# The conditional block moved ahead of the last slot's scalings and scatters, and that slot's rows transposed by TensorE

## The chip, the cores and the metric

The kernel runs on one core of a Trainium2 chip. The metric is the device time of one execution in microseconds; of several executions the median is taken. A profiled execution also gives a span, from the first to the last instruction of the core, and a trace of that execution.

## What is computed

Attention with a causal mask and a decay bias runs over 8 batches of 8 heads (576 positions of 64 values). Its output, 4608 rows of 512 values, goes through a mixture of 16 experts (4 groups of 4), each of which has a hidden layer of 1024. A row goes to one expert, chosen by two argmax steps:

```python
x = attn_out.transpose(0, 2, 1, 3).reshape(B * S, H * D)      # 4608 x 512
g_idx = argmax(x @ w_group)                                   # group of a row, with softmax weight g_w
e_idx = argmax(x @ w_expert[g_idx])                           # expert in the group, with weight e_w
h = maximum(x_row @ w1[g, e], 0.0)                            # 512 -> 1024
out[row] = (g_w * e_w) * (h @ w2[g, e])                       # 1024 -> 512
```

## The kernel before

The first half of the execution is attention and routing; the change does not touch it. In the second half (`moe`) the 16 experts, sorted by how many rows they have, are handled in 16 slots, 0 to 15. A slot has a fixed capacity (`CAPS`): slot 13 has 264 rows, slots 14 and 15 have 256, so two tiles of 128 rows. Rows beyond a capacity go to the conditional block at the end, which is entered when the count `nov` is above zero. With these inputs it is not entered: no instruction of its body stands in the trace.

Each float32 matrix is split into a rounded high part and the low rest (`wh`, `wl`; `xh`, `xl`; `hh`, `hl`), and a product is three matmuls. A slot has these steps:

- `gather`: GpSimd fetches the slot's rows from DRAM into `xg` by an indirect DMA, long ahead.
- `x_items`: the rows are transposed and split into `xh` and `xl`. Slots 0 and 1 do it on TensorE, into PSUM (lines 1040 to 1045). All later slots do it on VectorE: 16 transposes of 32-row blocks into `xt` (line 1059), then a cast on ScalarE (`xh`, line 1063) and a subtraction on VectorE (`xl`, line 1064) for each half.
- `h_items`: 8 pieces of 12 matmuls (line 1092), each followed by `hh` on ScalarE (line 1087) and `hl` on VectorE (line 1088).
- `y_items`: where the capacity is a multiple of 128, `y_rows` (lines 1105 to 1124): 4 pieces of 12 matmuls of 512 columns (line 1114), two pieces to a tile of 128 rows. Behind the second piece of a tile VectorE scales the tile by the row's weight (line 1121), and GpSimd scatters it into the output (line 943).
- `z_items`: for other capacities, 16 transposes on VectorE (line 1200), three scalings on ScalarE (line 1203) and three scatters. They run during the next slot's `h_items`, and the scalings stand behind all 16 transposes.
- `load`: 16 pieces for the next slot's weights, with casts on ScalarE (lines 982 and 990) and subtractions on GpSimd (985) and VectorE (992).

Each engine runs its instructions in the order in which they stand. In the loop over the slots (lines 1433 to 1447) the order on TensorE, VectorE and ScalarE is the order of the code: pieces of the next slot's `x_items` and `load` stand between the pieces of this slot. GpSimd's and the DMA queues' order is the scheduler's. PSUM tiles come from two pools, `acc` for products and `turn_in` for transposes and casts; `turn_in` has four buffers, used in turn.

Behind the loop stands the block: every engine loads `nov` into a register (line 1449), compares and branches (line 1450). On the path around the body each engine raises its own semaphores by what the body would have raised them; GpSimd does this also for the eight semaphores of its DMA queue (`INC_SWDGE_SEM`). Behind it comes the end of the program: the Sync engine waits for all DMAs, and all five engines meet in a barrier, for which GpSimd first runs a `DRAIN`.

Of the kernel before, what the change touches and what calls it, by code (L numbers as in the profile page):

```python
# [13 lines left out]
ALU = mybir.AluOpType  # L14
# [8 lines left out]
DM = 512  # L23
FF = 1024
E = 16
# [883 lines left out]
def moe(tc, w1, w2, xs, st, out):  # L909
# [3 lines left out]
    with ExitStack() as ctx:  # L913
# [27 lines left out]
        def scatter(y, ids, free=False):  # L941

            i = nc.gpsimd.indirect_dma_start(out=out, in_=y, in_offset=None, bounds_check=NTOK - 1, oob_is_err=False,  # L943
                                             out_offset=bass.IndirectOffsetOnAxis(ap=ids, axis=0))
            if free:
                tc.declare_no_dep(i.ins, group="rows", reason="distinct rows")
                tc.add_to_no_dep_group("rows", i.ins)
# [52 lines left out]
        def turn_in(name, dt=F32):  # L1000

            n = turned_in[0] = turned_in[0] + 1
            return pt[n > 6 and n % 4 == 3].tile([P, 512], dt, name=name, tag="pt")
# [18 lines left out]
        class Slot:  # L1022
# [12 lines left out]
            def x_items(self):  # L1035
                u, cap = self.u, self.cap
                self.xh, self.xl = xhl(u, 0 if u == 0 else u + 1)

                def item(c):
                    ps = acc(f"px{u}_{c}") if u == 0 else turn_in(f"px{u}_{c}")  # L1040
                    for t, r in enumerate(self.rows):
                        nc.tensor.transpose(ps[:, t * P:t * P + r], self.xg[:r, t, c * P:(c + 1) * P], ident[:r, :r])
                    self.split = (nc.scalar.copy(self.xh[:, c, :cap], ps[:, :cap]),
                                  V.tensor_tensor(out=self.xl[:, c, :cap], in0=ps[:, :cap],
                                                  in1=self.xh[:, c, :cap].bitcast(F32), op=ALU.subtract))

                if u < 2:
                    return [lambda c=c: item(c) for c in range(4)]

                xt = turned(u)  # L1050
                nb = -(-cap // 32)

                def turn(j, i0):

                    n = len(range(j, nb, 4))
                    for i in (i0, i0 + 1):
                        src = self.xg[32 * j:32 * j + 32].rearrange("p t (c i n) -> p t c i n", c=4, n=32)
                        dst = xt[32 * i:32 * i + 32].rearrange("p c (t j n) -> p t c j n", j=4, n=32)
                        V.transpose(dst[:, 0:n, :, j], src[:, 0:n, :, i])  # L1059

                def split(a):
                    xh, xl, x = (t[:, a:a + 2, :cap] for t in (self.xh, self.xl, xt))
                    nc.scalar.copy(xh, x)  # L1063
                    V.tensor_tensor(out=xl, in0=x, in1=xh.bitcast(F32), op=ALU.subtract)  # L1064

                return ([lambda j=j, i=i: turn(j, i) for j in range(4) for i in (0, 2)] +
                        [lambda a=a: split(a) for a in (0, 2)])
# [37 lines left out]
            def y_rows(self):  # L1105

                pss, yr = {}, {}

                def item(t, f0):
                    if f0 == 0:  # L1110
                        pss[t] = acc(f"py{self.u}_{t}")
                    for f in range(f0, f0 + 4):
                        for n, (x, w) in enumerate(((self.hh, self.w.h), (self.hh, self.w.l), (self.hl, self.w.h))):
                            nc.tensor.matmul(pss[t], x[:, f, t * P:(t + 1) * P], w[2 + f // 4][:, f % 4],
                                             start=(f == 0 and n == 0), stop=(f == 7 and n == 2))
                    if f0 == 4:
                        if t == 0:
                            yr[0] = rows(self.u) if self.u % 2 else yT.rearrange("p c t -> p (c t)").rearrange(
                                "p (t d) -> p t d", d=DM)
                        yo = yr[0][:, t]  # L1120
                        V.tensor_scalar(out=yo, in0=pss[t], scalar1=self.cw[:, t:t + 1], scalar2=None, op0=ALU.mult)
                        scatter(yo, self.ids[:, t:t + 1], True)

                return [lambda t=t, f=f: item(t, f) for t in range(len(self.rows)) for f in (0, 4)]

# [83 lines left out]
        class Tile:  # L1209
# [8 lines left out]
            def items(self):  # L1218
# [17 lines left out]
                def hidden(i, c0):  # L1236
                    if c0 == 0:

                        pss[i] = turn_in(f"pu{u}_{i}") if u == "r" else acc(f"pu{u}_{i}")
                    for c in range(c0, c0 + 2):  # L1240
                        for n, (a, b) in enumerate(((th, w.h), (tl, w.h), (th, w.l))):
                            nc.tensor.matmul(pss[i], a[:, c, 0:P], b[i][:, c], start=(c == 0 and n == 0),
                                             stop=(c == 3 and n == 2))
                    if c0 == 2:
                        nc.scalar.activation(h[:, i * 512:(i + 1) * 512], pss[i], AF.Relu)
# [4 lines left out]

                def y(f0):
                    if f0 == 0:
                        pss["y"] = acc(f"pv{u}")
                    for f in range(f0, f0 + 2):
                        fs = slice(P + P * (f % 2), 2 * P + P * (f % 2))
                        for n, (a, b) in enumerate(((th, w.h), (tl, w.h), (th, w.l))):
                            nc.tensor.matmul(pss["y"], a[:, f // 2, fs], b[2 + f // 4][:, f % 4],
                                             start=(f == 0 and n == 0), stop=(f == 7 and n == 2))
                    if f0 == 6:
                        yo = rows(u)[:, 0]  # L1260
                        V.tensor_scalar(out=yo, in0=pss["y"], scalar1=self.cw, scalar2=None, op0=ALU.mult)
                        scatter(yo, self.ids)
# [171 lines left out]
        with tc.manual_schedule(engines={ENG.PE, ENG.DVE, ENG.Activation}):  # L1434
            for k in range(1, E):
                W = wts[k + 1].load() if k + 1 < E else []
                for i, f in enumerate(slots[k].h_items()):
                    f()
                    run(Z[i:i + 1] + W[i:i + 1])
                    if i == 4 and k + 2 < E:  # L1440
                        slots[k + 2].gather()
                X = slots[k + 1].x_items() if k + 1 < E else []
                for i, f in enumerate(slots[k].y_items()):
                    run((Z[8:] if i == 0 else []) + X[4 * i:4 * i + 4] + W[8 + 2 * i:10 + 2 * i])
                    f()
                Z = slots[k].z_items()
            run(Z)

        nov = nc.values_load(spilli[0:1, 3:4], min_val=0, max_val=2 * E)  # L1449
        with tc.If(nov > 0):  # L1450
# [54 lines left out]
            with tc.If(nge > 0):  # L1505
# [50 lines left out]
                with tc.For_i(0, nge, 1) as i:  # L1556
# [8 lines left out]
                    run(w.load())  # L1565
                    run(o.items())


def _layout(inputs):
    import numpy as np  # L1570
# [41 lines left out]
```

## Time and profile before

| | us |
|---|---|
| median of 3 runs (lowest, highest) | 950.84 (948.24, 955.85) |
| the profiled execution | 953.42 |
| its span | 951.7 |
| TensorE busy | 869.3 (91% of the span) |
| VectorE busy | 747.3 (79%) |
| ScalarE busy | 609.0 (64%) |
| GpSimd busy | 606.6 (64%) |

The mean granted TensorE clock is 0.963 of full speed. Busy times are summed over the whole span; the change concerns its last 55 us. Times in rows are microseconds from the start of the span. A number in square brackets at the end of a row is the idle time of that engine just ahead of the instruction, with what ended it. Rows whose engine name ends in "q" are instructions that an engine's queue handles itself (branches, register loads, semaphores, drains); they do not count as busy.

### The profile page before, as it was taken

How to read it: one execution, taken by the hardware profiler on the slowest of the kernel's cores; microseconds unless marked ns; L12 is line 12 of the kernel's file. 1: busy time of each engine (PE TensorE's matmuls, PEld its weight loads, DVE VectorE, ACT ScalarE, POOL GpSimd, SP SyncE). 2: the span in 40 equal slices, each digit the busy share in tenths (PEclk: the TensorE clock that was granted, in tenths of full speed). 3: DMA queues.
4: the chain of work that ended last, by engine and by line, in shares of the span. 5: the costliest groups of instructions: out<-in, count | busy, mean ns of one | idle time of the engine just before them, and what ended most of it. 6: DMA issues, size and time to landing. Idle time of an engine off the chain costs nothing. (4 is left out here: it accounts for less than half of the span.)

```text
span 951.7 us, 17736 instructions
## 1 busy us (share of the span) xinstructions
PE 869.3 (91%) x5576; PEld 792.1 (83%) x5576; DVE 747.3 (79%) x1996; ACT 609.0 (64%) x1383; POOL 606.6 (64%) x748
## 2 busy tenths in 40 slices
PE   4889899999899999999695999999999999999983
PEld 3678788888788888887584999999999999999972
DVE  7546688787988788775599678898888889888850
ACT  5458668677767767775634556767677666676640
POOL 9647567666666757546675557666676777676630
PEclk9979999999999999998797999999999999999997
DMA  7999989989999989712536345556555555565410
GB/s 189 229 196 225 221 213 227 221 200 200 212 210 213 216 213 226 175 57 103 196 125 212 137 160 190 186 167 223 185 200 188 205 190 176 212 223 208 145 43 23
DMA packets 82165, 174.65 MB, mean 184 GB/s; under 512 B 9708, under 2 KB 45164, under 8 KB 73872
## 3 DMA queue, kind: packets, MB, share of 16 engines
q1 hardware_dynamic: 71952, 153.52, 58.7%
q0 software_dynamic: 7488, 18.89, 5.6%
q10 hardware_dynamic: 2624, 1.03, 0.5%
q8 instruction: 46, 0.75, 0.4%
q14 instruction: 55, 0.45, 0.2%
HBM read 108.97 MB, written 19.69 MB: 135 GB/s over the span
## 5 line engine op out<-in xcount | busy, mean ns | idle before, releaser
L985 POOL TENSOR_TENSOR wl<-raw,wh 128x512 fp32r<-128x512 f32 x163 | 209.9, 1300 | 76.0 <-ACT wh L982 57.3
L221 DVE CUSTOM_DVE_ANT_0 mx<-pm,mask 128x192 bf16<-128x192 f32 (+4 forms) x320 | 127.5, 419 | 46.7 <-PE pm L213 44.1
L982 ACT CAST wh<-raw 128x512 fp32r<-128x512 f32 x256 | 155.2, 616 | 11.6 <-issue 11.6
L1092 PE MATMUL ph<-xl,wh 128*128 128x256 f32 (+13 forms) x512 | 146.7, 306 | 4.0 <-DVE xl L1064 4.0
L1092 PE MATMUL ph<-xh,wh 128*128 128x256 f32 (+13 forms) x512 | 145.8, 303 | 3.9 <-ACT xh L1063 3.8
L213 PE MATMUL pm<-WA 66*128 66x288 f32 (+4 forms) x384 | 127.8, 364 | 22.6 <-DVE mc L221 12.0
L269 PE MATMUL ps<-WA 68*128 68x320 f32 (+4 forms) x384 | 138.4, 364 | 3.0 <-ACT pu L279 1.9
L309 PE MATMUL po<-pt,VT 128*128 128x256 f32 (+3 forms) x512 | 123.8, 362 | 8.1 <-ACT sums L316 6.8
L1147 PE MATMUL py<-hl,wh 128*128 128x256 f32 (+13 forms) x448 | 113.7, 302 | 1.9 <-DVE hl L1088 1.9
L1147 PE MATMUL py<-hh,wh 128*128 128x256 f32 (+13 forms) x448 | 112.8, 301 | 0.0
L1059 DVE STREAM_TRANSPOSE xt<-xg 32x256 f32<-32x256 f32 (+1 forms) x224 | 109.4, 489 | 3.4
L271 PE MATMUL ps<-WB 128*128 128x320 f32 (+4 forms) x384 | 112.0, 305 | 0.0
L309 PE MATMUL po<-pu,VT 128*128 128x320 f32 (+1 forms) x384 | 109.7, 395 | 0.3 <-POOL pu L288 0.3
L309 PEld LDWEIGHTS po<-pt,VT 128*128 128x128 f32 x512 | 91.0, 198 | 22.4 <-issue 9.3
L1200 DVE STREAM_TRANSPOSE yr<-yT 32x384 f32<-32x384 f32 (+1 forms) x208 | 104.5, 502 | 4.3
L1092 PEld LDWEIGHTS ph<-xl,wh 128*128 128x128 f32 x512 | 98.1, 192 | 7.1 <-DVE xl L1064 6.1
L1092 PEld LDWEIGHTS ph<-xh,wh 128*128 128x128 f32 x512 | 98.0, 191 | 6.1 <-ACT xh L1063 5.8
L288 POOL TENSOR_SCALAR_AFFINE_SELECT pt<-pt 128x128 f32<-128x128 f32 (+2 forms) x192 | 66.3, 356 | 53.8 <-ACT pt L279 51.3
L213 PEld LDWEIGHTS pm<-WA 66*128 66x128 f32 (+1 forms) x384 | 71.2, 197 | 33.5 <-DVE mc L221 16.7
L1087 ACT ACTIVATE hh<-ph 128x256 fp32r<-128x256 f32 (+13 forms) x128 | 53.8, 420 | 59.2 <-PE ph L1092 58.3
L371 POOL TENSOR_TENSOR xTl<-xT,xTh 128x512 fp32r<-128x512 f32 x30 | 38.2, 1273 | 83.4 <-ACT xTh L367 64.1
L155 POOL TENSOR_TENSOR WB<-r,hl 64x576 fp32r<-64x576 f32 x62 | 87.9, 1418 | 5.3 <-ACT hl L151 2.8
(248 smaller groups left out, 2071.1 us busy)
## 6 DMA issues: line engine op xcount, KB each, us to landing
raw<-in_w_dram SPq DMA_DIRECT2D x64, 1024.0 KB
r<-in_qk_dram SPq DMA_DIRECT2D x32, 576.0 KB
WA<-hl SPq DMA_DIRECT2D x61, 288.0 KB
WB<-hl SPq DMA_DIRECT2D x61, 288.0 KB
VT<-in_v_dram SPq DMA_DIRECT2D x32, 384.0 KB
WB<-hl SPq DMA_DIRECT2D x64, 144.0 KB
xs<-xr SPq DMA_DIRECT2D x15, 512.0 KB
WA<-cumd SPq DMA_DIRECT2D x56, 4.5 KB
```

The costliest lines, as they stand in the source:

```text
L155: (nc.vector if p < 1 else nc.gpsimd).tensor_tensor(out=hl[:, 2] if part else WB[p % NBB][0:64, KA, h], in0=r[hr, part], in1=hl[hr, part]. ...
L213: nc.tensor.matmul(ps[:rows, :cw], WA[i][0:66, QA, h, QO + q0:QO + q0 + rows], WA[i][0:66, KA, h, QO + c0:QO + c0 + cw], start=True, stop= ...
L221: nc.vector.tensor_tensor_reduce(out=tmp[:rows, :cw], in0=ps[:rows, :cw], in1=mk[:rows], scale=1.0, scalar=-3.0e38 if c0 == 0 else mo, op0 ...
L269: nc.tensor.matmul(ps[:rows, o:o + w], WA[i][0:68, KA, h, QO + k0:QO + k0 + rows], WA[i][0:68, QA, h, QO + q0:QO + q0 + w], start=True, st ...
L271: nc.tensor.matmul(ps[:rows, o:o + w], WB[p % NBB][:, KA, h, k0:k0 + rows], WB[p % NBB][:, QA, h, q0:q0 + w], start=False, stop=True)
L309: nc.tensor.matmul(po[0][:, qa - base:qb - base], VT[p % NVT].rearrange("p t a d -> p (t a d)")[:, (3 * t + 1 + h) * 64:][:, 0:P], x[:, c: ...
L982: self.casts.append(nc.scalar.copy(h[:, j], raw[:, j]))
L985: self.low = lows[self.u, i, j] = nc.gpsimd.tensor_tensor(out=l[:, j], in0=raw[:, j], in1=h[:, j].bitcast(F32), op=ALU.subtract)
L1059: V.transpose(dst[:, 0:n, :, j], src[:, 0:n, :, i])
L1092: self.product = nc.tensor.matmul(pss[f][:, :cap], w[f // 4][:, c, (f % 4) * P:(f % 4 + 1) * P], x[:, c, :cap], start=(c == 0 and w is sel ...
L1147: self.product = nc.tensor.matmul(pss[c][:, :cap], w[2 + f // 4][:, f % 4, c * P:(c + 1) * P], x[:, f, :cap], start=(f == 0 and w is self. ...
L1200: V.transpose(dst[:, 0:n, :, i], src[:, 0:n, :, j])
```

## The change

Three things change in the code that runs.

1. For the last slot `x_items` takes the way of slots 0 and 1: TensorE transposes 128x128 blocks into PSUM, two for each of four column blocks, ScalarE casts each block of 256 columns, VectorE subtracts. In slot 14's `y_items` one such piece stands ahead of each of the four pieces; before, ten pieces stood 4, 4, 2 and 0.
2. In `y_rows` the last slot no longer scales and scatters at once. The two calls are kept in a list, `self.leave`, that is run behind the conditional block. The scaled rows go into `yT` instead of a tile of their own.
3. Two PSUM tiles of the block's body change pools. That body does not run here.

```diff
-                if u < 2:
+                if u < 2 or u == E - 1:
                     return [lambda c=c: item(c) for c in range(4)]
...
+                self.leave = []
...
-                        yo = yr[0][:, t]
-                        V.tensor_scalar(out=yo, in0=pss[t], scalar1=self.cw[:, t:t + 1], scalar2=None, op0=ALU.mult)
-                        scatter(yo, self.ids[:, t:t + 1], True)
+                        if self.u == E - 1:
+                            self.leave.append(lambda: leave(t, yT.rearrange("p c t -> p (c t)")[:, t * DM:(t + 1) * DM]))
+                        else:
+                            leave(t, yr[0][:, t])
+
+                def leave(t, yo):
+                    V.tensor_scalar(out=yo, in0=pss[t], scalar1=self.cw[:, t:t + 1], scalar2=None, op0=ALU.mult)
+                    scatter(yo, self.ids[:, t:t + 1], True)
...
                 for i, f in enumerate(slots[k].y_items()):
-                    run((Z[8:] if i == 0 else []) + X[4 * i:4 * i + 4] + W[8 + 2 * i:10 + 2 * i])
+                    n = 1 if k + 2 == E else 4
+                    run((Z[8:] if i == 0 else []) + X[n * i:n * i + n] + W[8 + 2 * i:10 + 2 * i])
                     f()
...
+        run(slots[E - 1].leave)
```

On GpSimd the scatters change places with the block. Before, its rows at the end of the main program are these (`yT` holds slot 14's rows, `yr15` slot 15's; the last row is the first of the block's body):

```order
L943 DMA out_0_dram<-yT_6563,ids_6566 4608x512
L943 DMA out_0_dram<-yr15_12246,ids_6566 4608x512 x2
L1449 TENSOR_LOAD spilli_7187
L1450 COMPARE_AND_BRANCH
L938 DMA xg0_6561<-xs_60,spilli_7187 128x512
```

After the change they are these (`L1457 ISA` closes the block, and `L1617` is the end of the program):

```order
L943 DMA out_0_dram<-yT_6563,ids_6566 4608x512
L1456 TENSOR_LOAD spilli_7187
L1457 COMPARE_AND_BRANCH
...
L1457 ISA
L1457 UNCONDITIONAL_BRANCH
L943 DMA out_0_dram<-yT_6563,ids_6566 4608x512 x2
L1617 UNCONDITIONAL_BRANCH
L1617 ISA
```

GpSimd now goes through the block right behind slot 14's last scatter, and both scatters of slot 15 are its last work. On VectorE the scheduler places the first of the two scalings still ahead of the block's register load, and the second behind the block.

On TensorE, after the change, the transposes stand between the pieces of slot 14's second product (`ph14` is its first product, `py14` its second by tile, `px15` the transposed rows of slot 15; each "..." leaves out the rest of 12 matmuls of a piece). Before, no row stood between the pieces:

```order
L1092 MATMUL ph14_7_11961<-xh14_11632,wl14_1_11459 128x256 x4
L1042 MATMUL px15_0_11994<-ident_61,xg1_6562 128x128 x2
L1115 MATMUL py14_0_12006<-wh14_2_11461,hh14_11820 128x512
...
L1042 MATMUL px15_1_12019<-ident_61,xg1_6562 128x128 x2
L1115 MATMUL py14_0_12006<-wh14_3_11464,hh14_11820 128x512
...
L1042 MATMUL px15_2_12046<-ident_61,xg1_6562 128x128 x2
L1115 MATMUL py14_1_12058<-wh14_2_11461,hh14_11820 128x512
...
L1042 MATMUL px15_3_12071<-ident_61,xg1_6562 128x128 x2
L1115 MATMUL py14_1_12058<-wh14_3_11464,hh14_11820 128x512
```

So a piece of `py14` cannot start until the transposes ahead of it have their PSUM buffer. `px15_2` takes the buffer of `px15_0`, and waits for VectorE's subtraction out of it; `px15_3` waits in the same way for that of `px15_1`.

On ScalarE the casts of `x` before stood behind six weight casts:

```order
L1203 ACTIVATE yr13_11797<-yr13_11797,cws_6567 8x512
L982 CAST wh15_2_11815<-raw15_2_11814 128x512
L990 CAST pw15_2_0_12005<-raw15_2_11814 128x512
L982 CAST wh15_2_11815<-raw15_2_11814 128x512 x2
L990 CAST pw15_2_2_12032<-raw15_2_11814 128x512
L982 CAST wh15_2_11815<-raw15_2_11814 128x512
L1063 CAST xh15_11980<-xt15_11982 128x2x256 x2
```

Now the first stands right behind slot 13's three scalings (`yr13`), and the others follow after three weight casts each:

```order
L1209 ACTIVATE yr13_11797<-yr13_11797,cws_6567 8x512
L1043 CAST xh15_11980<-px15_0_11994 128x256
L982 CAST wh15_2_11815<-raw15_2_11814 128x512
L990 CAST pw15_2_0_12001<-raw15_2_11814 128x512
L982 CAST wh15_2_11815<-raw15_2_11814 128x512
L1043 CAST xh15_11980<-px15_1_12019 128x256
```

VectorE's rows change in the same way: its 16 transposes and two subtractions become four subtractions of 256 columns, between the weight subtractions.

## Rows read from the trace of the kernel before

**Rows 1.** The page's head, whole execution.

```profile
span 951.7 us, 17736 instructions
```

**Rows 2.** POOL in order of time, its last two scatters: start, us, instruction.

```profile
931.85 0.98 POOL L943 DMA_INDIRECT out_dram<-yr,ids  x1 [14.84 <-DVE yr L1121]
937.29 0.97 POOL L943 DMA_INDIRECT out_dram<-yr,ids  x1 [4.46 <-DVE yr L1121]
```

**Rows 3.** Lines 1449, 1450: queue instructions; ns min/median/max, first and last start.

```profile
L1449 POOLq TENSOR_LOAD <-spilli x1: 507/507/507, 937.1 to 937.1; - x1
...
L1450 POOLq EVENT_SEMAPHORE  x6: 17/30/43, 940.7 to 941.1; - x6
...
L1450 ACTq EVENT_SEMAPHORE  x2: 17/17/17, 928.4 to 928.5; - x2
...
L1450 ACTq COMPARE_BRANCH  x1: 54/54/54, 925.9 to 925.9; - x1
...
L1450 POOLq COMPARE_BRANCH  x1: 62/62/62, 937.6 to 937.6; - x1
L1450 POOLq INC_SWDGE_SEM  x1: 2028/2028/2028, 941.2 to 941.2; - x1
```

**Rows 4.** Line 1608, the program's end: POOLq of the span, SPq and DRAIN in 936:945.

```profile
L1608 POOLq EVENT_SEMAPHORE  x4: 17/17/17, 950.9 to 951.6; - x4
...
L1608 SPq EVENT_SEMAPHORE  x12: 28/28/28, 943.2 to 943.9; - x12
...
L1608 POOLq DRAIN  x1: 7582/7582/7582, 943.3 to 943.3; - x1
```

**Rows 5.** Line 1601, the start of the program: GpSimd's other DRAIN.

```profile
L1601 POOLq DRAIN  x1: 187/187/187, 0.4 to 0.4; - x1
```

**Rows 6.** Line 943 in 931 to 945 us: from a scatter's issue to its landing.

```profile
DMA to landing us min/median/max: 3.3/4.0/4.7
```

**Rows 7.** PE in order of time around slot 15's first product.

```profile
897.63 0.40 PE L1114 MATMUL py<-wh,hh 128*128 128x512 f32 x1
...
910.91 0.38 PE L1092 MATMUL ph<-xh,wh 128*128 128x256 f32 x1 [2.21 <-ACT xh L1063]
912.25 0.58 PE L1092 MATMUL ph<-xl,wh 128*128 128x256 f32 x1 [0.95 <-DVE xl L1064]
...
925.15 0.40 PE L1114 MATMUL py<-wh,hh 128*128 128x512 f32 x1
```

**Rows 8.** Stretches: us; PE, PEld, DVE, ACT, POOL busy (instructions); PEclk; DMA share; GB/s.

```profile
897.60:908.70 11.10, 11.10 (x50) 8.86 (x48) 10.69 (x24) 5.96 (x11) 7.04 (x7) 1.00 0.31 123
912.00:915.40 3.40, 3.15 (x15) 3.15 (x15) 2.75 (x5) 2.85 (x6) 3.21 (x3) 0.51 0.22 82
```

**Rows 9.** ACT in order of time around slot 13's scalings, and its last `hh`.

```profile
902.38 1.95 ACT L1203 ACTIVATE yr<-yr,cws 128x512 f32<-128x512 f32 x3 [3.66 <-issue]
904.24 0.60 ACT L982 CAST wh<-raw 128x512 fp32r<-128x512 f32 x1
...
925.35 0.38 ACT L1087 ACTIVATE hh<-ph 128x256 fp32r<-128x256 f32 x1 [1.06 <-PE ph L1092]
```

**Rows 10.** DVE in order of time: the first eight of slot 15's transposes.

```profile
902.33 3.58 DVE L1059 STREAM_TRANSPOSE xt<-xg 32x256 f32<-32x256 f32 x8
```

**Rows 11.** Slots 0 and 1: PE in order of time; lines 1043, 1044 with ns min/median/max.

```profile
498.73 0.48 PE L1042 MATMUL px<-ident,xg 128*128 128x128 f32 x3
...
L1043 ACT CAST xh<-px x4: 363/373/378, 464.5 to 465.4; 128x256 fp32r<-128x256 f32 x4
...
L1044 DVE TENSOR_TENSOR xl<-px,xh x4: 414/420/425, 464.9 to 465.9; 128x256 fp32r<-128x256 f32 x4
```

**Rows 12.** Two earlier stretches in which TensorE idled, in the columns of rows 8.

```profile
188.40:195.20 6.80, 5.32 (x20) 4.05 (x19) 5.31 (x16) 2.19 (x6) 2.03 (x3) 0.75 0.69 170
482.00:488.80 6.80, 5.27 (x45) 5.07 (x44) 6.67 (x21) 3.15 (x6) 5.87 (x8) 1.00 0.51 153
```

More of the change, by code (lines that the diff above doesn't have):

```diff
@@ L1116, in item @@
                     if f0 == 4:
-                        if t == 0:
+                        if t == 0 and self.u < E - 1:
                             yr[0] = rows(self.u) if self.u % 2 else yT.rearrange("p c t -> p (c t)").rearrange(
                                 "p (t d) -> p t d", d=DM)
-                        yo = yr[0][:, t]
-                        V.tensor_scalar(out=yo, in0=pss[t], scalar1=self.cw[:, t:t + 1], scalar2=None, op0=ALU.mult)
-                        scatter(yo, self.ids[:, t:t + 1], True)
+                        if self.u == E - 1:
[5 more added lines that the diff above has]
+                    scatter(yo, self.ids[:, t:t + 1], True)
                 return [lambda t=t, f=f: item(t, f) for t in range(len(self.rows)) for f in (0, 4)]
@@ L1237, in hidden @@
                     if c0 == 0:
-                        pss[i] = turn_in(f"pu{u}_{i}") if u == "r" else acc(f"pu{u}_{i}")
+                        pss[i] = turn_in(f"pu{u}_{i}")
                     for c in range(c0, c0 + 2):
@@ L1252, in y @@
                     if f0 == 0:
-                        pss["y"] = acc(f"pv{u}")
+                        pss["y"] = acc(f"pv{u}") if u == "r" else turn_in(f"pv{u}")
                     for f in range(f0, f0 + 2):
```

## The prediction

> **What bounds the kernel now.** I read the profile from its end. The span ends at 951.7 us [rows 1], but the last scatter's instruction is over at 938.26 (937.29 + 0.97) [rows 2]. So 13.4 us at the end hold no computation. The queue rows of the block and of the program's end fill them, all on GpSimd [rows 3, 4]. Its branch stands at 937.6 and the next instruction of its queue at 940.7, so 3.1 us pass between them. Six semaphore instructions follow until 941.1, then `INC_SWDGE_SEM` from 941.2 for 2.03 us [rows 3]. Then comes a `DRAIN` from 943.3 for 7.58 us, and the barrier, 950.9 to 951.6 with the span's end at 951.7: 0.8 us [rows 4]. The other engines' parts of this are over earlier.
>
> The second place is slot 15's start, which I read in TensorE's order of time [rows 7]. Slot 14's second product begins at 897.63 and TensorE is busy until 908.70 (910.91 - 2.21), so it takes 11.07 us. Then TensorE waits 2.21 us for `xh` and, one matmul later, 0.95 us for `xl`. The reason is VectorE: it is busy 10.69 of the 11.10 us of the stretch 897.6 to 908.7 [rows 8], and slot 15's first eight transposes start only at 902.33 [rows 10], behind slot 13's.
>
> Slot 15's first product lasts from 910.91 to 925.15, 14.24 us [rows 7]. Undisturbed it is 8 x 1.44 = 11.52 us, where 1.44 is the length of one `hh` and the wait for the next (0.38 + 1.06) [rows 9]. The 0.95 us of waiting is in the 14.24, and 14.24 - 0.95 - 11.52 = 1.77 us are left. They are the clock's: the granted clock is 0.51 in 912.0 to 915.4 [rows 8], which is the level of 1.2 GHz, right behind the idle time.
>
> **The change, part 1: slot 15's rows.** What goes is the two waits and the slow clock, 2.21 + 0.95 + 1.77 = 4.93 us.
>
> What comes is eight transposes on TensorE. Three of them took 0.48 us, the last one's own 0.27 included, so about 0.11 us apart [rows 11]: 8 x 0.11 = 0.88 us. All of it is on the path, since TensorE has no idle time left there.
>
> A wait comes too. The transposes of `px15_2` need the subtraction out of `px15_0`, and the whole second tile of slot 14 is queued behind them on TensorE. That subtraction needs the first cast, which stands on ScalarE behind slot 13's three scalings. ScalarE's next instruction after these began at 904.24 [rows 9]. A cast of 256 columns takes 0.37 us and the subtraction 0.42 [rows 11], which makes 905.03, and about 905.1 with the hand-overs. TensorE gets there at 897.63 + 4 x 0.11 + 11.07 / 2 = 903.6. It waits 1.5 us.
>
> What stands behind is covered. `px15_3` needs the second subtraction: with three weight casts of 0.60 [rows 9] and a cast of 0.37 it is done by 904.24 + 0.37 + 1.80 + 0.37 + 0.42 = 907.2, and TensorE asks at 905.1 + 0.22 + 2.77 = 908.1. The last cast is done by 904.24 + 4 x 0.37 + 9 x 0.60 = 911.1, its subtraction by 911.5. TensorE begins the first product at 905.1 + 0.44 + 5.54 = 911.1 and asks for the last `xl` seven matmuls (0.8 us) later. The cover is 0.4 us, and if it is gone TensorE waits for the rest. VectorE's rows in that time (four subtractions of 0.42, some weight subtractions and a scaling) are far fewer than the 16 transposes that it loses, 3.58 us for each eight [rows 10].
>
> So part 1 is worth 4.93 - 0.88 - 1.5 = 2.5 us, if the clock holds over the 1.5 us of waiting. Two stretches of this trace bound that. In 188.4 to 195.2 TensorE idled 1.48 us and the granted clock has a mean of 0.75, so it was at the lower level for half of it. In 482.0 to 488.8 it idled 1.53 us and the clock stayed at 1.00 [rows 12]. If it falls, it costs the 1.77 us again, and part 1 is worth 0.8 us. I take 2.5, slightly the likelier one, and keep 0.8 as the other bound.
>
> **Part 2: the block under slot 15's products.** Between the last scatter's end, 938.26, and the `DRAIN`, 943.3, lie 5.0 us. They hold the branch, the semaphores and `INC_SWDGE_SEM`. After the change GpSimd does all this, with its register load 6.1 us (937.1 to 943.2) [rows 3], behind slot 14's last scatter. There it idles for 14.84 us [rows 2], of which part 1 takes 2.5: it is hidden with 6.2 us to spare. Without that cover it would be back on the path.
>
> VectorE has the block between its two scalings. The scatters, and so the scalings, are 5.44 us apart [rows 2], which leaves 4.7 us behind a scaling of 0.75. ScalarE took 2.5 us from its branch to its next instruction (925.9 to 928.4), GpSimd 3.1 [rows 3]. Even with 3.1 and a register load of 0.5 VectorE is in time. Nothing else that is on the path is queued behind these branches. So part 2 is worth 5.0 us.
>
> **What the end costs then.** The last scatter starts at 937.29 - 2.5 = 934.8 and is over at 935.8. The `DRAIN` is now right behind it. Its length is the great unknown. The trace has only one such drain behind scatters, 7.58 us, and it began when nothing was left that the trace shows: the scatter had landed at 937.29 + 3.3 = 940.6 [rows 6]. So I take 7.58 again: 935.8 + 7.6 + 0.8 = 944.2 for the span. The Sync engine waits for the scatter's landing (934.8 + 3.3 to 4.7 [rows 6]) and goes through its semaphores, but this ends before 941 and is hidden by the drain.
>
> **The sum.** 951.7 - 2.5 - 5.0 = 944.2 us of span. The profiled execution took 953.42, so 945.9 for one like it. It lies 2.58 us above the median; from the median of 950.84 the forecast is **943.3 us**, 0.8% less. About 1%, 9.5 us, is what a measurement of this kernel can tell from no change.
>
> **The rivals.**
>
> *The drain was `INC_SWDGE_SEM`'s.* The 7.58 us may be work that this instruction left behind in GpSimd; the drain at the program's start, which had only small fills ahead of it, took 0.19 us [rows 5]. Then it is hidden too, and the Sync engine sets the end: landing at 934.8 + 3.3 = 938.1, about 0.8 us for its semaphores (943.2 to 943.9 before), and the barrier's 0.8, so 939.7 of span. That is 12.0 us less, 938.9. Against it: all eight semaphores had been raised when the Sync engine went through them from 943.2 on [rows 4], so the instruction's visible work was over. The Trainium skill, VectorE: DVE Perf Modes, section The DRAIN you can't avoid, calls the drains at a program's start and end about 12 ns long on all five engines; by that a drain has no length of its own and this rival's 938.9 follows. The trace disagrees for GpSimd with 7.58 us.
>
> *Part of the 5.0 us is the scatter's landing.* The last scatter landed at 937.29 + 3.3 = 940.6 [rows 6], and GpSimd's queue went on at 940.7 [rows 3]. On the path around the body it waits for that landing anyway, before `INC_SWDGE_SEM`. If the drain waits for it too, only 943.3 - 940.6 = 2.7 us are gained at the end, and the time is 950.84 - 2.5 - 2.7 = 945.6. Against it: ScalarE also took 2.5 us to get on, and waited for no scatter; so most of the 3.1 us is the branch itself. The Trainium skill, Advanced Engine Details and Errata, section Control Flow Timing, gives a compare-and-branch about 108 ns; by that the gap was the landing's and this rival's 945.6 follows. The trace has 2.5 and 3.1 us behind the two branches, which is what the Trainium skill, Runtime: NRT & Kernel Launch, section Instruction fetch mechanics, expects where a branch leaves the prefetched window.
>
> *The drain's end hangs on the last scatter.* From the scatter's start to the drain's end it was 13.56 us (937.29 to 950.85). If that is fixed, part 2 brings nothing, since the block stood in a wait that remains: 950.84 - 2.5 = 948.3. For it speaks that scatters are GpSimd's only outstanding work; against it that this one had long landed.
>
> *Slower: the drain meets a scatter in flight.* Before, the drain began 2.7 us behind the landing; now it begins 2.3 us ahead of it, which no row shows. If its work starts only with the landing and then takes the 13.56 us, it ends at 938.1 + 13.56 = 951.7, the span is 952.5, and the time 951.6. From a drain of 15.1 us (7.58 + 7.5) on, the change loses.
>
> *The clock falls at the new wait.* 943.3 + 1.7 = 945.0, as above.
>
> **How the numbers follow.** The forecast with the clock holding has 0.30, with the clock falling 0.22. The hidden drain has 0.14 (938.9, or 940.6 with a fall), the landing 0.14 (945.6 or 947.3), the fixed end 0.14 (948.3 or 950.0), the drain in flight 0.03; 0.03 is for what I don't see. The range from 938.5 to 949.0 leaves out the last two and the fixed end with a falling clock, about 0.12, and some of what scatters around 938.9. Faster by over 1% means under 941.3: nearly all of the hidden drain, and about 0.1 of the forecast's cases, since single executions before lie up to 5 us from their median; 0.23. Slower by over 1% means over 960.3: 0.02. The rest, 0.75, is within 1%.
>
> **What would show it.** TensorE's wait for `xh` at the start of slot 15's first product is gone, and one of about 1.5 us stands ahead of `px15_2`, with VectorE's subtraction as its end. The stretch from slot 14's second product to slot 15's second product is about 25.0 us, not 27.5. GpSimd's `INC_SWDGE_SEM` stands some 10 us ahead of slot 15's first scatter, and its `DRAIN` within 0.2 us of the last scatter's end, 7.6 us long. The prediction is wrong if the drain has another length, if the wait at `px15_2` is much over 2 us, or if VectorE's second scaling starts late because of its branch.

## The result, and the profile after

The changed kernel takes 943.21 us (median of 17 runs), the kernel before 951.25 us (17 runs on the same chips). The ratio is 0.9913 with a 95% interval of 0.989 to 0.9937: 8.0 us less, 0.8%. That is within the 1% that the text above calls no change, but with 17 runs of each kernel the interval lies wholly below 1, so the gain is clear of the noise. The forecast was 943.3.

The head of the page of the kernel after gives a span of 10.1 us less than [rows 1]:

```profile
span 941.6 us, 17740 instructions
```

TensorE in order of time (start, us, instruction, and in brackets the idle time ahead of it with what ended it). The first two rows here are the transposes ahead of the first and the third piece of slot 14's second product:

```profile
894.98 0.38 PE L1042 MATMUL px<-ident,xg 128*128 128x128 f32 x2
...
902.45 0.44 PE L1042 MATMUL px<-ident,xg 128*128 128x128 f32 x2 [1.34 <-DVE xl L1044]
...
908.49 0.28 PE L1092 MATMUL ph<-xh,wh 128*128 128x256 f32 x1
...
920.00 0.40 PE L1115 MATMUL py<-wh,hh 128*128 128x512 f32 x1
```

Against [rows 7], the two waits at slot 15's first product are gone: its first row, at 908.49, has no bracket. One new wait of 1.34 us stands ahead of the third pair of transposes. From slot 14's second product to slot 15's second product it is 920.00 - 894.98 = 25.02 us, where it was 27.52.

The same stretch in three pieces (us; busy time and instructions of PE, PEld, DVE, ACT, POOL; granted clock; DMA share; GB/s):

```profile
894.98:902.45 7.47, 6.13 (x30) 4.72 (x29) 4.91 (x11) 3.60 (x8) 3.71 (x4) 1.00 0.28 118
902.45:908.49 6.04, 6.04 (x28) 4.96 (x29) 3.95 (x8) 6.04 (x15) 5.51 (x6) 1.00 0.19 73
908.49:920.00 11.51, 11.51 (x97) 11.51 (x96) 4.28 (x9) 3.17 (x8) 3.06 (x3) 1.00 0.12 46
```

The granted clock is 1.00 in all three. The level of 0.51 of [rows 8] does not come back, and slot 15's first product takes 11.51 us. VectorE, busy 10.69 of 11.10 us in [rows 8], is now busy 4.91 + 3.95 = 8.86 of 13.51.

GpSimd in order of time at the end: slot 14's last scatter and the two of slot 15.

```profile
910.71 1.00 POOL L943 DMA_INDIRECT out_dram<-yT,ids  x1 [0.17 <-issue]
926.70 0.97 POOL L943 DMA_INDIRECT out_dram<-yT,ids  x1 [14.99 <-DVE yT L1127]
932.14 0.97 POOL L943 DMA_INDIRECT out_dram<-yT,ids  x1 [4.47 <-DVE yT L1127]
```

The block (lines 1456 and 1457 now; ns min/median/max, first and last start in us), and the program's end (line 1617) in 926 to 940.8 us:

```profile
L1456 POOLq TENSOR_LOAD <-spilli x1: 502/502/502, 909.8 to 909.8; - x1
...
L1457 POOLq EVENT_SEMAPHORE  x6: 17/30/43, 913.2 to 913.7; - x6
...
L1457 DVEq EVENT_SEMAPHORE  x2: 21/21/21, 926.9 to 927.0; - x2
...
L1457 POOLq COMPARE_BRANCH  x1: 62/62/62, 910.4 to 910.4; - x1
L1457 POOLq INC_SWDGE_SEM  x1: 1988/1988/1988, 913.8 to 913.8; - x1
...
L1457 DVEq COMPARE_BRANCH  x1: 72/72/72, 926.3 to 926.3; - x1
```

```profile
L1617 SPq EVENT_SEMAPHORE  x12: 27/28/19256, 915.7 to 935.6; - x12
...
L1617 POOLq DRAIN  x1: 8790/8790/8790, 931.9 to 931.9; - x1
```

GpSimd goes through the block from 910.4 to 915.8, and slot 15's first scatter starts 10.9 us later: the block is hidden. The queue takes up the `DRAIN` at 931.9, ahead of the scatter's own record, so its row is longer than that of [rows 4]. What counts is its end: 940.69, which is 7.58 us behind the last scatter's end at 933.11. From the scatter's end to the span's end it is 8.5 us, where it was 13.4.

So the stretch gives 2.5 us and the end 5.0. The other 2.65 us of the span lie ahead of the change's place: slot 14's second product begins at 894.98 instead of 897.63. The profiled executions below put that point anywhere from 887.7 to 898.7 (890.5 in the kernel before with one drain added behind that point), so this is a difference between executions.

### The profile page after: what moved, and what is told of

Same layout as the page of the kernel before. It is cut to its first block, busy times and chain, and to the rows that moved or that the text cites. A ratio compares the mean times of both kernels' runs of the same rounds, so it can differ in the third digit from the quotient of the medians.

```text
span 941.6 us, 17740 instructions
## 1 busy us (share of the span) xinstructions
PE 867.2 (92%) x5584; PEld 790.9 (84%) x5584; DVE 739.8 (79%) x1982; ACT 608.5 (65%) x1385; POOL 606.0 (64%) x748
## 5 line engine op out<-in xcount | busy, mean ns | idle before, releaser
L1059 DVE STREAM_TRANSPOSE xt<-xg 32x256 f32<-32x256 f32 (+1 forms) x208 | 102.5, 493 | 3.1
```

## The experiments

Single executions of one kernel differ by more than 10 us, and the timed ratios have intervals of 2 to 6 us to either side. Steps of one or two us are therefore read from two stretches within each execution. *Stretch* runs from slot 14's second product (its first pair of transposes, where TensorE has them) to slot 15's second product. *Tail* runs from the last scatter's end to the span's end. Between the two lie 13.1 us in each of these executions. Each number is from one profiled execution; kernels that share a stage agree within about 0.1 us in it.

| kernel | stretch, us | tail, us | ratio to before (95%) |
|---|---|---|---|
| before | 27.52 | 13.4 | |
| after | 25.02 | 8.5 | 0.9913 (0.989 to 0.9937) |
| after, once more | 25.01 | 8.5 | 0.9882 (0.9827 to 0.9937) |
| part 1 alone | 25.00 | 13.4 | 0.9958 (0.9928 to 0.9988) |
| part 2 alone | 27.51 | 8.5 | 0.9927 (0.9894 to 0.9961) |
| first cast earlier | 23.58 | 8.5 | 0.9911 (0.9883 to 0.994) |
| casts later | 26.55 | 8.5 | 0.994 (0.9906 to 0.9973) |
| early drain | 24.99 | 3.3 | 0.9838 (0.978 to 0.9895) |
| first cast earlier, early drain | 23.59 | 3.3 | 0.9862 (0.9807 to 0.9918) |
| before with early drain | 27.40 | 4.5 | 0.9933 (0.989 to 0.9976) |

The kernel after was run a second time, beside others.

> The changed kernel itself once more, beside the others of this call: 8.0 us under the kernel before, ratio 0.991.

It has the stretch and the tail of the first time (25.01 and 8.5 us), and a ratio whose interval holds the 0.991.

### Each part alone

Part 1 alone, the kernel after with the scalings and scatters back in their place:

```diff
-                        if t == 0 and self.u < E - 1:
+                        if t == 0:
...
-                        if self.u == E - 1:
-                            self.leave.append(lambda: leave(t, yT.rearrange("p c t -> p (c t)")[:, t * DM:(t + 1) * DM]))
-                        else:
-                            leave(t, yr[0][:, t])
+                        leave(t, yr[0][:, t])
...
-        run(slots[E - 1].leave)
```

> Part 1 alone: slot 15's rows are transposed by TensorE in four pieces, and its scalings and scatters stand ahead of the conditional block as before. My theory: the stretch from the start of slot 14's second product to the start of slot 15's second product is 25.0 us (27.5 before), and the end of the program is that of before: branch, six semaphores, INC_SWDGE_SEM and DRAIN all behind the last scatter, 13.4 us from the last scatter's end to the span's end. Time 2.5 us under the kernel before, 0.3%. Rival, that the two parts only work together because GpSimd and VectorE are relieved of the block: the stretch stays above 26 us. Rival, that the end shrinks with the earlier finish of TensorE: less than 12.5 us behind the last scatter.

TensorE's stretch is 914.38 - 889.38 = 25.00 us, with a wait of 1.31 us ahead of the third pair of transposes. GpSimd's last scatter (order of time), and the end (lines 1457 and 1617):

```profile
926.51 0.97 POOL L943 DMA_INDIRECT out_dram<-yr,ids  x1 [4.47 <-DVE yr L1127]
```

```profile
L1457 POOLq INC_SWDGE_SEM  x1: 2028/2028/2028, 930.4 to 930.4; - x1
...
L1617 POOLq DRAIN  x3: 46/107/7582, 932.5 to 940.6; - x3
```

`INC_SWDGE_SEM` with 2.03 us and the `DRAIN` with 7.58 are behind the scatter, as in [rows 3, 4]. Part 1 gives its 2.5 us without part 2, and nothing at the end.

Part 2 alone, the kernel after with slot 15's rows transposed by VectorE again:

```diff
-                if u < 2 or u == E - 1:
+                if u < 2:
...
-                    n = 1 if k + 2 == E else 4
+                    n = 4
```

> Part 2 alone: the conditional block stands ahead of slot 15's scalings and scatters, and VectorE transposes slot 15's rows as before. My theory: the stretch from slot 14's second product to slot 15's second product is 27.5 us as before, with the waits of about 2.2 and 1.0 us at slot 15's first product and the granted clock at its lower level (1.2 GHz) for some us behind them; the last scatter's end to the span's end is 8.5 us (13.4 before), with a DRAIN that ends 7.6 us behind the last scatter's end. Time 5.0 us under the kernel before, 0.5%. Rival, that part of the 5.0 us is only gained because part 1 moves the scatters: 9.5 us or more behind the last scatter.

TensorE in order of time, and the stretch behind it in the columns of the windows above:

```profile
903.64 0.38 PE L1092 MATMUL ph<-xh,wh 128*128 128x256 f32 x1 [2.24 <-ACT xh L1063]
904.97 0.58 PE L1092 MATMUL ph<-xl,wh 128*128 128x256 f32 x1 [0.94 <-DVE xl L1064]
```

```profile
905.00:908.00 3.00, 3.00 (x14) 3.00 (x15) 2.41 (x4) 2.45 (x6) 2.81 (x3) 0.50 0.25 93
```

The waits and the slow clock of [rows 7, 8] are back, and the tail is that of the kernel after. The two parts are independent and add: 2.5 and 5.0 us.

### The place of the first cast

The first of slot 15's casts on ScalarE goes ahead of slot 13's three scalings:

```diff
-                    run((Z[8:] if i == 0 else []) + X[n * i:n * i + n] + W[8 + 2 * i:10 + 2 * i])
+                    run(X[n * i:n * i + n] * (n == 1) + (Z[8:] if i == 0 else []) + X[n * i:n * i + n] * (n == 4) + W[8 + 2 * i:10 + 2 * i])
```

> The changed kernel, with slot 15's first cast ahead of slot 13's three scalings on ScalarE. If the wait of 1.34 us ahead of the third pair of transposes is the place of that cast, as the prediction has it, the first subtraction runs by about 900.1, before TensorE asks at 901.1; the wait goes, the stretch from slot 14's second product to slot 15's second product falls from 25.02 to 23.7 us, and the time is 1.3 us under the changed kernel, about 9.3 us under the kernel before. Rival, that VectorE (behind slot 13's transposes) is the bound: the wait shrinks by less than half. Rival, that the time goes into a wait for the last xl at slot 15's first product: the stretch stays above 24.5 us.

TensorE in order of time, the first and the third pair of transposes, and VectorE's first subtraction:

```profile
887.68 0.38 PE L1042 MATMUL px<-ident,xg 128*128 128x128 f32 x2
...
893.67 0.38 PE L1042 MATMUL px<-ident,xg 128*128 128x128 f32 x2
```

```profile
892.39 0.43 DVE L1044 TENSOR_TENSOR xl<-px,xh 128x256 fp32r<-128x256 f32 x1
```

The third pair has no wait. The subtraction is over at 892.82, before TensorE asks, and the stretch is 23.58 us, 1.44 less. So the wait of the kernel after was ScalarE's order and nothing else. The ratio of this kernel cannot be told from that of the kernel after; the stretch can.

The opposite edit puts each cast behind the three weight casts of its piece:

```diff
-                    run((Z[8:] if i == 0 else []) + X[n * i:n * i + n] + W[8 + 2 * i:10 + 2 * i])
+                    run((Z[8:] if i == 0 else []) + X[n * i:n * i + n] * (n == 4) + W[8 + 2 * i:10 + 2 * i] + X[n * i:n * i + n] * (n == 1))
```

> The changed kernel, with each of slot 15's four casts behind the three weight casts of its piece on ScalarE instead of ahead of them, which puts the first one about 1.6 us later. The wait ahead of the third pair of transposes goes from 1.34 to about 2.9 us. If TensorE's clock stays at 2.4 GHz over such a wait, the stretch from slot 14's second product to slot 15's second product is 26.6 us. If the clock falls, as it did behind the wait of 2.21 us in the kernel before, the granted clock is near 0.5 for some us behind the wait and the stretch is 28.3 us.

TensorE in order of time, and three windows of the stretch:

```profile
906.77 0.44 PE L1042 MATMUL px<-ident,xg 128*128 128x128 f32 x2 [2.94 <-DVE xl L1044]
```

```profile
897.74:906.77 9.03, 6.09 (x30) 4.71 (x28) 5.60 (x12) 5.16 (x11) 4.97 (x5) 1.00 0.36 146
906.77:912.78 6.01, 6.01 (x29) 4.96 (x30) 3.98 (x7) 4.97 (x12) 5.57 (x6) 1.00 0.03 12
912.78:924.29 11.51, 11.51 (x98) 11.51 (x96) 3.73 (x8) 2.69 (x7) 1.77 (x2) 1.00 0.12 46
```

The wait is 2.94 us, the clock stays at 2.4 GHz (1.00), and the stretch is 26.55 us: the wait costs its own length and no more.

### What the DRAIN waits for

The 7.58 us of the `DRAIN` are the largest term left, and the prediction had one row for them. Four of the kernels of this section ran only once (three copies, no scatters, one copy, the drain in the middle), so only their rows are read, not their times. The first two kernels ask whether they belong to the last scatter. The one puts three copies behind it:

```diff
-        run(slots[E - 1].leave)
+        run(slots[E - 1].leave + [lambda y=yT.rearrange("p c t -> p (c t)"): nc.gpsimd.tensor_copy(y[:, 2 * DM:3 * DM], y[:, DM:2 * DM])] * 3)
```

> The changed kernel, with three copies of a 128x512 tile on GpSimd behind the last scatter (into a part of a tile that nothing reads), about 1.0 to 1.4 us each. If the DRAIN takes its 7.58 us behind whatever GpSimd did last, its end moves by the length of the copies, 3 to 4 us, and stands 7.6 us behind the end of the last copy. If the 7.58 us belong to the last scatter's instruction, the copies lie inside them: the DRAIN still ends 7.6 us behind the last scatter's end, and the span is that of the changed kernel.

GpSimd in order of time, and line 1617:

```profile
931.18 0.97 POOL L943 DMA_INDIRECT out_dram<-yT,ids  x1 [4.47 <-DVE yT L1127]
932.14 1.98 POOL L1575 COPY yT<-yT 128x512 f32<-128x512 f32 x3
```

```profile
L1617 POOLq DRAIN  x3: 46/113/8242, 933.5 to 942.3; - x3
```

The copies were shorter than expected, 1.98 us together. The drain ends at 933.5 + 8.24 = 941.7, 7.6 us behind the last copy (934.12). The price is paid behind whatever GpSimd did last.

The other leaves slot 15's scatters out:

```diff
-                    scatter(yo, self.ids[:, t:t + 1], True)
+                    scatter(yo, self.ids[:, t:t + 1], True) if self.u < E - 1 else None
```

> The changed kernel without slot 15's two scatters: the 256 rows of that slot are scaled but not written. GpSimd's last work is then slot 14's last scatter (ends at about 911.7) and the block, with INC_SWDGE_SEM to about 915.8, and its DRAIN stands right behind. If the DRAIN has its own length of 7.58 us behind anything, it ends at about 923.4. If the 7.58 us belong to the last scatter, it ends at about 919.3, 3.5 us long. If they need both a scatter and nothing behind it, it is short, and ends at about 916. In all cases it is hidden, and the span ends about 1 us behind VectorE's second scaling, near 933.

Lines 1457 and 1617:

```profile
L1457 POOLq INC_SWDGE_SEM  x1: 1988/1988/1988, 908.9 to 908.9; - x1
...
L1617 POOLq DRAIN  x3: 46/107/7418, 910.9 to 928.0; - x3
```

The drain stands right behind the block at 910.9, takes 7.42 us there and is hidden. It needs no scatter just ahead of it. The tail behind VectorE's second scaling (927.14) is 1.1 us. That left two readings: a price of each drain, or something that has piled up. One more drain in GpSimd's idle time tells them apart (`scatter` returns its instruction for that, and the drain is issued behind slot 14's last one):

```diff
+            return i
...
-                    scatter(yo, self.ids[:, t:t + 1], True)
+                    self.sent = scatter(yo, self.ids[:, t:t + 1], True)
...
             run(Z)
+        with after(tc, slots[E - 2].sent): nc.gpsimd.drain()
```

> The changed kernel with one more drain of GpSimd, behind slot 14's last scatter and ahead of the block, in GpSimd's idle time. It takes about 7.5 us there and moves GpSimd's way through the block to about 919.3 to 925.4, still ahead of slot 15's first scatter at 926.7. If the final DRAIN's 7.58 us are a price of each drain that has some work ahead of it, the final one is 7.6 us behind the last scatter again and the time is that of the changed kernel. If they are work that has piled up over the program (or code that is fetched once), the early drain takes it, the final one is short, and the end is set by the Sync engine behind the scatter's landing: about 5 us less than the changed kernel, 938.

Lines 1455 (the early drain), 1457 and 1617:

```profile
L1455 POOLq DRAIN  x1: 9297/9297/9297, 904.8 to 904.8; - x1
...
L1457 POOLq EVENT_SEMAPHORE  x6: 17/30/43, 917.6 to 918.1; - x6
...
L1457 POOLq COMPARE_BRANCH  x1: 62/62/62, 914.8 to 914.8; - x1
...
L1457 POOLq INC_SWDGE_SEM  x1: 189/189/189, 918.1 to 918.1; - x1
...
L1617 SPq EVENT_SEMAPHORE  x14: 17/28/11474, 918.3 to 931.3; - x14
...
L1617 POOLq DRAIN  x3: 46/113/2985, 926.9 to 931.1; - x3
```

The early drain ends at 914.1, 7.4 us behind slot 14's last scatter (906.72). Then `INC_SWDGE_SEM` takes 0.19 us instead of 1.99, and the final `DRAIN` ends at 929.9 instead of 928.08 + 7.58 = 935.7. The Sync engine's wait for the last scatter's landing ends at 918.3 + 11.47 = 929.8, so the drain ends about 0.1 us behind the landing, and the tail is 3.3 us. So not each drain has this price; the early one has paid it. Whether it is work that piled up or something that is paid only once, this run does not tell. With the same early drain and one copy in place of slot 15's scatters, whose rows are then not written, there is no landing to wait for:

> The same early drain, and in place of slot 15's two scatters (its 256 rows are scaled but not written) one copy of a 128x512 tile on GpSimd behind the last scaling, 0.7 us. If a drain costs 7.5 us behind any work of GpSimd, the final DRAIN ends 7.6 us behind the copy. If only scatters make it long, the final DRAIN ends within 0.3 us of the copy's end. If the early drain takes it all, likewise; then the other run of this pair tells the two apart.

GpSimd's copy, and line 1617:

```profile
927.50 0.60 POOL L1575 COPY yT<-yT 128x512 f32<-128x512 f32 x1 [20.21 <-DVE yT L1127]
```

```profile
L1617 POOLq DRAIN  x3: 34/113/710, 927.5 to 928.8; - x3
```

The copy ends at 928.10 (927.50 + 0.60), and the longest of the final drains, 0.71 us, begins at 927.5 and ends at 928.2. Behind an early drain neither work of another kind nor the drain itself has a price.

What piles up? Two sizes suggested it: 7.58 us behind 92 indirect DMAs (46 gathers and 46 scatters) and 7.42 us behind 90, both 0.0824 us each; the early drain, also behind 90, took 7.42 us too (914.145 - 906.725). `INC_SWDGE_SEM` fits 0.19 us and 0.020 for each. A drain in the middle of the slots is the test:

```diff
                     if i == 4 and k + 2 < E:
                         slots[k + 2].gather()
+                        with after(tc, slots[k + 2].last): nc.gpsimd.drain() if k == 7 else None
```

> The changed kernel with one more drain of GpSimd, not at the end but behind the gather of slot 9, where 45 of the 92 gathers and scatters have been issued. Theory: a drain works off 0.0824 us for each indirect DMA since the drain before it (7.58 us for 92, 7.42 us for 90 so far), and INC_SWDGE_SEM takes 0.19 us and 0.020 us for each (2.03, 1.99 and 0.19 us for 92, 90 and 0). Then this drain ends 3.7 us behind its gather's end, INC_SWDGE_SEM takes 0.19 + 45 x 0.020 = 1.09 us, and the final DRAIN ends 47 x 0.0824 = 3.9 us behind the last scatter's end. Rival: the length is paid once, by the first drain behind a long stretch (code that is fetched): the drain here has 7.4 us, and the final one ends 1.8 us behind the last scatter's end, as behind the early drain at the end. Rival: it counts all of GpSimd's instructions: the final DRAIN has about 7.58 x the share of GpSimd's instructions behind slot 9's gather, 0.31, so 2.4 us.

GpSimd in order of time, then lines 1448 (the drain in the middle), 1457 and 1617:

```profile
684.48 0.95 POOL L938 DMA_INDIRECT xg<-xs,ids x1 [0.30 <-issue]
...
929.35 0.97 POOL L943 DMA_INDIRECT out_dram<-yT,ids  x1 [4.47 <-DVE yT L1127]
```

```profile
L1448 POOLq DRAIN  x1: 6892/6892/6892, 683.1 to 683.1; - x1
...
L1457 POOLq INC_SWDGE_SEM  x1: 1088/1088/1088, 910.8 to 910.8; - x1
...
L1617 POOLq DRAIN  x3: 46/113/5110, 929.1 to 934.8; - x3
```

`INC_SWDGE_SEM` takes 1.088 us where 1.09 was expected. The final drain ends at 934.21, 3.89 us behind the last scatter's end, where 47 x 0.0824 = 3.87. Both rivals (1.8 and 2.4 us) fall. A third, that the rows moved count and not the DMAs, had no kernel of its own, but these rows speak against it. By the slots' capacities (`CAPS`) 4,630 to 4,800 of 9,728 rows lie behind the drain in the middle, so by rows the final drain would be 3.6 to 3.7 us and `INC_SWDGE_SEM`, which has slot 15's 256 rows still to come, 1.02 to 1.05; this is an estimate. The drain in the middle itself ends 4.56 us behind its gather, 0.85 more than 45 x 0.0824 = 3.71. A wait for that gather's landing does not explain it: in the trace the raises of the gather's semaphore end at 688.15, 1.9 us ahead of the drain's end. Of the two scatters just ahead of the gather the trace has only some of the raises, so this stays open.

The same drain in the kernel before shows what part 2 covered:

```diff
+            return i
...
-                        scatter(yo, self.ids[:, t:t + 1], True)
+                        self.sent = scatter(yo, self.ids[:, t:t + 1], True)
...
                     if i == 4 and k + 2 < E:
                         slots[k + 2].gather()
+                    if i == 4 and k == E - 1:
+                        with after(tc, slots[k - 1].sent): nc.gpsimd.drain()
```

> The kernel before, with one drain of GpSimd added behind slot 14's last scatter, and nothing else: the block still stands behind slot 15's scatters, and VectorE transposes slot 15's rows. By the price for each indirect DMA the INC_SWDGE_SEM takes 0.23 us instead of 2.03, the final DRAIN is short (0.1 to 0.2 us instead of 7.58), and from the last scatter's end to the span's end 4.6 us pass (13.4 before): 8.8 us under the kernel before, more than the whole change brings. If the final DRAIN needs its 7.58 us behind the block in any case: 1.8 us under the kernel before.

Lines 1451 (the block) and 1609 (the end):

```profile
L1451 POOLq INC_SWDGE_SEM  x1: 235/235/235, 933.7 to 933.7; - x1
...
L1609 POOLq DRAIN  x3: 46/107/218, 934.0 to 935.2; - x3
```

Against 2028 and 7582 ns of [rows 3, 4] these are 235 and 218, and the tail is 4.5 us instead of 13.4. By the tail, one drain in idle time brings the kernel before 8.9 us, more than the 7.5 us of the whole change. The timed ratio, 0.9933, has an interval that reaches from 0.2% to 1.1% less and holds the 0.9%. The times do not show this drain as worth more than the change: the two medians on the same chip, 942.38 and 941.03, lie closer than the intervals can tell apart.

The two edits that gained, together on the kernel after:

> The changed kernel with both edits that gained: slot 15's first cast ahead of slot 13's three scalings, and a drain of GpSimd behind slot 14's last scatter. 1.4 us by the stretch from slot 14's second product to slot 15's second product (23.6 us) and 5.2 us by the end (3.3 us from the last scatter's end to the span's end, 8.5 in the changed kernel): 6.6 us under the changed kernel, so a ratio of 0.985 to the kernel before. If the earlier scatter meets GpSimd still in the block (1.3 us less cover), up to 1.3 us of it are lost and slot 15's first scatter starts late.

Their diffs are those of the first cast and of the early drain. The stretch is 23.59 us and the tail 3.3, so 6.6 us less than the kernel after, as expected. GpSimd leaves the block at 926.9 and has its next scatter at 928.96, 2.1 us later. The ratio of 0.9862 holds the expected 0.985 in its interval, but cannot be told from that of the early drain alone, nor from the 0.9882 of the kernel after beside it (937.76 against 941.03 us, 3.3 us apart where the stages have 6.6). By the stages this is the fastest version here, 14.0 us under the kernel before (3.93 + 10.1).

## Why the prediction was right

**Part 1: right, 2.5 us forecast and 2.5 measured.** The step to the wait ahead of `px15_2` held in its cause: an earlier cast removes it (23.58 us). Its size was 1.34 instead of 1.5, since TensorE got there 6.13 us behind its first transposes and not 5.97. The transposes cost more than 0.88: from 894.98 to 908.49 it is 13.51 us, and without the wait and the 11.07 of the product 1.10 us are left. These two errors of about 0.2 us cancel. The cover for the last `xl` was larger than the 0.4 us reckoned, since weight casts followed each other at 0.52 us, not 0.60. The first product's 11.51 us are the 11.52 of the working.

**The clock: the likelier case came true, but its reason is not settled.** Behind 1.34 us of idle time the clock stayed at 1.00, and behind 2.94 us as well. Yet behind 2.24 and 0.94 us at slot 15's first product it fell to 0.50. So the length of a wait alone does not tell which will happen. The two places differ in more than that: the one has a single wait inside slot 14's second product, the other two waits, one matmul apart, where slot 15's first product begins. No run here separates these.

**Part 2: right, 5.0 us forecast and 5.0 measured.** Part 2 alone has it too, so it hangs on nothing in part 1. The spare time for the block was 10.9 us, not 6.2. The working took part 1's 2.5 us from GpSimd's idle time, but slot 14's last scatter also came earlier: it ended 16.73 us behind the start of slot 14's second product (911.71 - 894.98), where it had been 19.38 (931.85 - 14.84 - 897.63). That is 2.65 us of the difference. The other 2.0 are a mis-sized term: the working set all 6.1 us of the block against the idle time, but GpSimd's queue took up the register load at 909.84, ahead of the scatter's own record, and only 4.1 us of the block lay behind the scatter's end (911.71 to 915.78). VectorE's branch took 0.6 us (926.3 to 926.9), less than the 3.1 allowed.

**The drain: the right size, for a reason that the prediction did not have.** It kept 7.58 us because that was the only row. The drain's length turned out to be the number of indirect DMAs behind it, 92 before and after, so the change could not alter it. That the only row was the right one to carry over was luck: nothing in the working shows why the length should stay. By its words the sign for the drain did not come true: the row stands at 931.9, ahead of the scatter, and is 8.79 us long; only its end, 7.58 us behind the scatter's, is as forecast. The rival of the hidden drain was right that it is work left behind. It was wrong on whose: the work is not `INC_SWDGE_SEM`'s, and GpSimd's idle time of 14.99 us does not work it off, only a drain does. The page named beside that rival (the Trainium skill, VectorE: DVE Perf Modes, section The DRAIN you can't avoid) gives drains at a program's end about 12 ns. Sync and ScalarE show such rows (7 to 13 ns at the end of the kernel after). For GpSimd the trace does not agree: 7.58 us, and 113 and 46 ns for the two short drains that follow.

**The other rivals.** That the 3.1 us of the branch were the scatter's landing falls: with the early drain GpSimd needs 2.8 us from its branch at 914.8 to its next instruction at 917.6, and no scatter was in flight there (slot 14's last had raised its semaphore by 908.5). The kernel after has 2.8 us too (910.4 to 913.2), but with a scatter in flight. And the 5.0 us came in full. That the end hangs on the scatter's start by 13.56 us falls: it was 940.69 - 932.14 = 8.55. That the drain begins its work only with the landing falls for the changed kernel too: the Sync engine's wait for the scatter ended at 934.98 (915.7 + 19.26), and the drain 5.7 us later, less than 7.58. Only where almost nothing is left to work off (early drain) does the landing set its end.

**The sum.** The forecast for the span, 944.2, missed the 941.6 by the 2.65 us that lie ahead of the change's place. The medians differ by 8.04 us, the forecast's 7.5. That the forecast of 943.3 and the median of 943.21 lie 0.1 us apart is chance: the interval of the ratio is over 2 us to either side, and the base of the forecast, 950.84, was the median of 3 runs where 17 have 951.25.

## What to carry to other kernels

A kernel that gathers and scatters through GpSimd's queue should try one drain of GpSimd in its last idle stretch, since the drain at the end otherwise pays for every indirect DMA of the program; here that is 8.9 us by the tail, where the change brings 7.5 by its stages, though the times cannot tell the two apart. Read a large fixed row at the end of a trace against what might be counted in it, such as instructions or DMAs, before taking it for a constant. And when a step moves to another engine, look at what its new neighbours in the queue are: three scalings ahead of one cast cost 1.4 us here, and a changed order of two list terms gave them back.

## What the runs showed of the hardware

GpSimd's drain and `INC_SWDGE_SEM`, by the number of indirect DMAs since the drain before:

| indirect DMAs since a drain | drain, us behind GpSimd's last work | `INC_SWDGE_SEM`, us |
|---|---|---|
| 92 (kernel before, part 1 alone) | 7.58 | 2.03 |
| 90 (without slot 15's scatters) | 7.42 | 1.99 |
| 90 (the early drain itself) | 7.42 | |
| 47 (drain in the middle, the final drain) | 3.89 | |
| 45 (the drain in the middle itself; the block later on) | 4.56 | 1.09 |
| 2, landed (before with early drain) | 0.22 | 0.235 |
| 2, the second in flight (early drain, the final drain) | 1.78 | |
| 0 (early drain, one copy; block behind it) | 0.08 | 0.19 |

That is 0.082 us for each in a drain and 0.020 in `INC_SWDGE_SEM`, wherever in the program the DMAs were issued and however long ago. Two drains took longer: the one in the middle by 0.85 us, which stays open, and the final one with a scatter in flight, which ended 0.1 us behind that scatter's landing, 2.75 us behind its start, in both kernels that have it. What GpSimd does for each indirect DMA is not shown by these traces, only that a drain does it and that it is then done.

TensorE's clock kept 2.4 GHz over a single wait of 2.94 us, which was not expected from the fall behind 2.21 and 0.95 us in [rows 7, 8].
